# Sinkhorn attention, a two-axis FFT, layer norm and an MLP on one core: loads in need order, a second folding of the transform, a GpSimd power, and transposes by the DMA crossbar

## The chip, the cores and the metric

The kernel runs on one core of one Trainium2 chip. The metric is the device time in microseconds (us) of that core. Every kernel here is timed in rounds beside the kernel before, on the same chip (another chip in another call), and all runs of this study agree within about 0.8% for one kernel. One more execution of each is profiled. Its span, from the first to the last instruction, is 1 to 2 us shorter than the time.

The engines are called PE (TensorE, matrix products; its weight loads are shown apart as PEld), DVE (VectorE), ACT (ScalarE), POOL (GpSimd) and SP (SyncE). A "q" behind an engine's name is its sequencer, as it issues a transfer.

## The reference, cut to what matters

```python
def _attn_ref(q, k, v, sort_net):            # q, k, v: 4 batches, 8 heads, 768 rows, 64
    P = sort_net                             # 4 x 8 matrices of 8 x 8
    for _ in range(5):                       # Sinkhorn
        P = exp(P - max(P, -1)); P = P / sum(P, -1); P = P / sum(P, -2)
    k_sorted = einsum('bhij,bhjcd->bhicd', P, k_blocks)
    v_sorted = einsum('bhij,bhjcd->bhicd', P, v_blocks)
    return softmax(q_blocks @ k_sorted.T / 8) @ v_sorted   # inside each block of 96

def _moe_ref(x, w_ch1, w_ch2):               # x: 4 x 768 x 512
    mixed = real(fft(fft(x, axis=1), axis=2))
    u = x + mixed
    un = (u - mean(u)) / sqrt(var(u) + 1e-6) # over the 512 of a row
    return u + maximum(un @ w_ch1, 0) @ w_ch2   # 512 x 2048 and 2048 x 512
```

One batch goes through it in this order: Sinkhorn, sorting of k and v, attention, first FFT axis, second FFT axis ("tiles" u of 128 rows, six to a batch), norm, MLP.

## The kernel before, where the change and the argument touch it

The Python of the kernel runs a few generators (attention, FFT, MLP, v of the later batches). The framework then orders each engine's instructions by a priority. An engine works strictly in that order, so an instruction that waits holds back all that stand behind it on the same engine.

A table of the second axis, `lt`, has 97 rows. Its two copies are loaded, and each is followed by a load of the single row 96 of `rb`. The table of the v correction (`tab`, f32) is loaded after them.

```python
    for n in range(2):
        lt = const.tile([97, S], F16, name=f"lt{n}")
        nc.sync.dma_start(lt, cn["lt"].ap())                # 97 rows; row 96 is written later
        rb = const.tile([97, DM], F16, name=f"rb{n}")
        nc.sync.dma_start(rb[96:97, :], cn["rrow"].ap())    # one row
    # ... cut ...
    tab = cload("tab", [128, 2, 2, 257], F32)
```

The second axis is one accumulation per tile, four matmuls of 512 columns and one with `lt` and `rb`:

```python
            ps = pf([128, DM])
            nc.tensor.matmul(ps, lt[:, 128 * T:128 * T + 128], rb, start=True, stop=False)
            for c in range(4):
                lh = ys[c][g][:, 128 * tt:128 * tt + 128]
                rh = cdb[:, c, :] if c < 2 else sdb[:, c - 2, :]
                nc.tensor.matmul(ps, lh, rh, start=False, stop=(c == 3))
```

The norm's inverse root is an integer first guess on DVE and three Newton steps on POOL, 15 small operations. Each normalised tile `un` is transposed by four PE matmuls and copied out of PSUM. The mean of v of batches 2 and 3 is subtracted on DVE by eight operations of 0.87 us. k and q go through two buffers each, and POOL issues their loads, so a new load waits on POOL until the old k or q has been used.

The softmax here doesn't subtract the row's maximum and nothing guards it: scores larger than these inputs give would overflow.

## Time and profile before

| | us |
|---|---|
| time, median of 4 runs beside the kernel after | 371.64 (370.59 to 373.28) |
| span of the profiled execution | 369.3 |
| table `tab` lands | 64.8 |
| first FFT's first operation | 88.8 |
| first MLP matmul | 129.6 |

The page of the profile, its row of busy tenths in 40 equal slices (9 is 90% or more; PEclk is the clock granted to PE, in tenths of full speed):

```profile
PE   0989500864885789999998999998999999999995
...
PEclk9998955775589699999999999999999999999999
DMA  8999987060335100514001101000100100100102
```

The matrix engine is full from slice 15 on and has holes before. The windows of the same trace, cut where the MLP starts (columns: window, length, busy time and count of PE, PEld, DVE, ACT, POOL, then clock, DMA share, GB/s):

```profile
0.00:129.60 129.60, 75.43 (x761) 53.40 (x762) 76.70 (x184) 57.90 (x102) 19.41 (x47) 0.78 0.65 139
129.60:369.30 239.70, 229.95 (x1695) 132.63 (x1692) 144.08 (x324) 80.61 (x148) 24.25 (x108) 1.00 0.11 33
```

After 129.6 us PE is busy for 230 of 240 us. Before, it is busy for 75 of 130. What it waited for there is in its waits (us in total, how often, the longest):

```profile
PE pf_575 L508 <- DMA tab_sb<-k_tab: 23.1, 1, 23.1
PE pm_139 L252 <- DMA v_82<-in_v_dram: 9.8, 1, 9.8
PE pf_1268 L704 <- ACT un_1250 L692: 5.5, 1, 5.5
PE pf_870 L636 <- DVE ee_834 L620: 5.3, 1, 5.3
```

The largest is the wait for `tab`. The timeline of SP's issues (start, duration, what) tells why it comes so late:

```profile
27.48 0.24 SPq L240 DMA_DIRECT2D lt_129<-k_lt  x1
27.77 7.63 SPq L243 DMA_DIRECT2D rb_131<-k_rrow  x1
35.44 1.06 SPq L240 DMA_DIRECT2D lt_133<-k_lt  x1
36.55 14.09 SPq L243 DMA_DIRECT2D rb_135<-k_rrow  x1
50.68 0.34 SPq L144 DMA_DIRECT2D tab_sb<-k_tab  x1
```

Two issues of one row took 7.6 and 14.1 us, and `tab` stands behind them.

### The profile page before, as it was taken

What the parts mean: (1) busy time and instruction counts of PE and PEld (TensorE: products, weight loads), DVE (VectorE), ACT (ScalarE), POOL (GpSimd) and SP (SyncE); (2) the same over time, 40 slices, a digit from 0 to 9 for tenths busy, and PEclk for the clock granted to TensorE, in tenths of its full rate; (3) what the DMA queues carried; (4) which work ended last, traced back from release to release, by engine and by line L of the source; (5) the groups of instructions that cost most, each with busy time, mean ns of one, the idle gap of its engine ahead of it and who ended that gap; (6) DMA issues with size and microseconds to landing.
All of it is one profiled execution on the core that took longest, in us unless ns stands there. A gap on an engine that the chain in (4) does not pass through costs nothing.

```text
span 369.3 us, 6087 instructions
## 1 busy us (share of the span) xinstructions
PE 305.4 (83%) x2452; PEld 186.0 (50%) x2452; DVE 220.8 (60%) x507; ACT 138.5 (38%) x249; POOL 43.7 (12%) x155
## 2 busy tenths in 40 slices
PE   0989500864885789999998999998999999999995
PEld 0448400752543667666643555664455555454552
DVE  3477500399988596447986644579473286563542
ACT  1647600371648688715302585630124212022100
POOL 7111000010004104000012300002011020021000
PEclk9998955775589699999999999999999999999999
DMA  8999987060335100514001101000100100100102
GB/s 155 320 265 225 210 219 250 27 105 0 44 45 66 22 0 6 83 57 78 9 0 58 41 2 51 36 2 0 59 28 3 58 28 2 57 30 28 57 2 85
DMA packets 18477, 25.95 MB, mean 70 GB/s; under 512 B 1737, under 2 KB 12685, under 8 KB 18449
## 3 DMA queue, kind: packets, MB, share of 16 engines
q0 software_dynamic: 11136, 10.49, 18.3%
q1 hardware_dynamic: 7314, 15.08, 11.5%
q8 instruction: 19, 0.31, 0.4%
q14 instruction: 8, 0.07, 0.1%
HBM read 29.37 MB, written 6.29 MB: 97 GB/s over the span
## 4 chain that ended last, share of the span: by engine, by line
PE 57%; DVE 19%; DMA 12%; SPq 7%; issue 2%; ACT 2%; POOL 1%; DVEq 0%; ACTq 0%
SPq L243 6%; DMA vcx<-k_sdb 4%; DMA tab_sb<-k_tab 4%; DMA v_82<-in_v_dram 2%; DVE vcx L873 2%; PE pm_3075 L773 1%; DVE r_540 L425 1%; PE pm_3013 L773 1%; PE pf_575 L508 1%; PE pm_2172 L773 1%; PE pm_2918 L773 1%; PE pm_4212 L773 1%; PE pm_2322 L773 1%; PE pm_3791 L773 1%; PE pm_4039 L773 1%
## 5 line engine op out<-in xcount | busy, mean ns | idle before, releaser
L756 PEld LDWEIGHTS <-w1sb 128*128 128x128 f16 x512 | 49.2, 98 | 36.6 <-issue 5.1
L508 PE MATMUL pf_575<-tab_sb,atp_537 128*64 128x129 f32 (+1 forms) x16 | 3.7, 405 | 23.1 <-DMA tab_sb<-k_tab 23.1
L465 PEld LDWEIGHTS <-vcx 128*128 128x128 f16 x128 | 18.1, 181 | 5.4 <-issue 2.3
L165 DVE CAST vsf<-pm_502 96x512 f16<-96x512 f32 x1 | 0.8, 799 | 27.7 <-PE pm_502 L468 27.7
L252 PE MATMUL pm_139<-v_82,idf_sb 128*128 128x512 f32 x12 | 7.7, 812 | 9.8 <-DMA v_82<-in_v_dram 9.8
L508 PEld LDWEIGHTS pf_575<-tab_sb,atp_537 128*64 128x64 f32 x16 | 3.1, 218 | 23.4 <-issue 23.4
L163 ACT CAST vsf<-pm_492 96x512 f16<-96x512 f32 x1 | 0.8, 786 | 25.2 <-PE pm_492 L468 25.2
L252 PEld LDWEIGHTS pm_139<-v_82,idf_sb 128*128 128x128 f32 x12 | 3.1, 267 | 13.6 <-issue 12.5
L468 PEld LDWEIGHTS <-vbn 128*128 128x128 f16 x64 | 8.7, 136 | 0.7 <-DVE bdv_1_291 L440 0.7
L773 PEld LDWEIGHTS <-hr_4077 128*128 128x128 f16 x48 | 4.7, 98 | 5.5
L773 PEld LDWEIGHTS <-hr_2224 128*128 128x128 f16 x48 | 4.7, 98 | 5.6
L773 PEld LDWEIGHTS <-hr_3663 128*128 128x128 f16 x48 | 4.7, 98 | 5.5
L773 PEld LDWEIGHTS <-hr_1704 128*128 128x128 f16 x48 | 4.6, 98 | 5.2
L773 PEld LDWEIGHTS <-hr_3127 128*128 128x128 f16 x48 | 4.6, 98 | 5.1
L773 PEld LDWEIGHTS <-hr_3898 128*128 128x128 f16 x48 | 4.6, 98 | 5.1
L692 ACT ACTIVATE un_3291<-u_2960,nm_3108,ny_3106 128x512 f16<-128x512 f32 x1 | 0.8, 813 | 16.8 <-POOL nm_3108 L680 16.8
L368 PEld LDWEIGHTS <-ksb_109 64*128 64x128 f16 x128 | 3.8, 97 | 6.5 <-issue 4.3
L413 PEld LDWEIGHTS <-ebuf_101 97*128 97x128 f16 x96 | 5.7, 108 | 2.6 <-DVE ebuf_101 L390 2.0
L692 ACT ACTIVATE un_2388<-u_2057,nm_2205,ny_2203 128x512 f16<-128x512 f32 x1 | 0.8, 813 | 16.5 <-POOL nm_2205 L680 16.5
L260 ACT CAST vcx<-v_82 128x768 f16<-128x768 f32 x4 | 3.3, 832 | 9.7 <-DMA v_82<-in_v_dram 9.7
L773 PEld LDWEIGHTS <-hr_3365 128*128 128x128 f16 x48 | 4.6, 98 | 4.5
L773 PEld LDWEIGHTS <-hr_2467 128*128 128x128 f16 x48 | 4.2, 98 | 4.7 <-issue 0.2
(1428 smaller groups left out, 896.4 us busy)
## 6 DMA issues: line engine op xcount, KB each, us to landing
w1sb<-in_moe_w_ch_dram POOLq DMA_DIRECT2D x4, 512.0 KB, 23.4
w2sb<-in_moe_w_ch_dram POOLq DMA_DIRECT2D x4, 512.0 KB, 32.3
v_82<-in_v_dram SPq DMA_DIRECT2D x4, 384.0 KB, 6.6
v_83<-in_v_dram SPq DMA_DIRECT2D x4, 384.0 KB, 13.2
v_524<-in_v_dram SPq DMA_DIRECT2D x2, 768.0 KB, 18.0
v_527<-in_v_dram SPq DMA_DIRECT2D x2, 768.0 KB, 18.9
tab_sb<-k_tab SPq DMA_DIRECT2D x1, 514.0 KB
k_70<-in_k_dram POOLq DMA_DIRECT2D x1, 384.0 KB, 5.6
```

Of the source, the lines that this page charges most:

```text
L243: nc.sync.dma_start(rb[96:97, :], cn["rrow"].ap())
L252: nc.tensor.matmul(psm.rearrange("p c d -> p (c d)"), idf, v32[n // 6][:, 8 * (n % 6):8 * (n % 6) + 8, :].rearrange("p c d -> p (c d)"), s ...
L260: nc.scalar.copy(vcp[:, 2 * n:2 * n + 2], v32[hf][:, 12 * qq:12 * qq + 12, :].rearrange("p (c r) d -> p c r d", r=6))
L368: nc.tensor.matmul(pss[h2][:, j, :], ks[rows, 4 * g + j].rearrange("p r c -> p (r c)"), qt[rows, :, cc])
L413: nc.tensor.matmul(po[:, 65 * T:65 * T + 96], e[:, S * g + 256 * tt + 128 * n: S * g + 256 * tt + 128 * n + 128], vsf[:, vi:vi + 96], star ...
L425: nc.vector.tensor_tensor(rt[:, :, D * h:D * h + D], po3[:, :, 0:D], rz[:, :, None].broadcast_to([128, 6, D]), op=ALU.mult)
L465: nc.tensor.matmul(ps[:, dd, :], vcx[:, :, d], bd, start=True, stop=(t == 1))
L468: nc.tensor.matmul(ps[:, dd, :], vbn[:, d:d + 1].broadcast_to([128, 128]), bd, start=False, stop=True)
L508: nc.tensor.matmul(psr[64 * o:64 * o + 64, cs], atp[:, par, c].rearrange("p b g -> p (b g)"), tab[:, o, c, cs], start=(c == 0), stop=(c == 1))
L756: nc.tensor.matmul(ps, w1sb[:, c, 128 * fc:128 * fc + 128], ut[:, c, :], start=(c == 0), stop=(c == 3))
L773: nc.tensor.matmul(ps, hr[:, fc, 128 * tt:128 * tt + 128], w2sb[:, fc, :], start=(fc == 0), stop=(fc == 15))
L873: nc.vector.tensor_tensor(vcp[:, 2 * n:2 * n + 2], v1[hf][:, 12 * qq:12 * qq + 12, :].rearrange("p (c r) d -> p c r d", r=6), vbs[1][:, 0: ...
```

## The change

The change has one aim, an earlier start of the MLP and fewer columns after it.

- Loads stand in the order of need: `tab` directly after v, both `lt` in one load and both `rb` rows in one, w1 between the two k and q loads of batch 1 and w2 behind them, and v of batches 2 and 3 in two pieces from POOL. Many instructions are given to `start(...)`, which keeps them at their place in program order.
- The mean of those later batches of v is subtracted by matmuls instead of on DVE, as for the first two already. v only needs a cast (ACT) and a tree of sums (DVE).
- The second axis is folded once more. A fold uses the symmetry of cosine and sine: mirrored inputs are added and subtracted first (on DVE), so that half as many products are left. Now even and odd output columns come from two matmuls of 256 columns each.
- The inverse root is one `pow` on POOL. Four operations replace 15.
- Rows of batches 1 to 3 are transposed by the DMA crossbar (a transfer that transposes on its way) instead of PE.
- Batch 1's attention waits until both groups of batch 0 are normalised.

```diff
+    load_qk(0, 1)
...
-    for n in range(8):
-        hf, qq = divmod(n, 4)
-        nc.sync.dma_start(v32[hf][:, 12 * qq:12 * qq + 12, :],
-                          vv[0:128, 12 * n:12 * n + 12, :])
+    for n in range(4):
+        hf, qq = divmod(n, 2)
+        start(nc.sync.dma_start(v32[hf][:, 24 * qq:24 * qq + 24, :],
+                                vv[0:128, 24 * n:24 * n + 24, :]))
...
+    start(nc.sync.dma_start(tab, cn["tab"].ap()))
+    start(nc.sync.dma_start(dtab, cn["dtab"].ap()))
+    start(nc.sync.dma_start(cs, cn["cs"].ap()))
+    lt2 = const.tile([97, 2, S], F16, name="lt2")
+    start(nc.sync.dma_start(lt2, cn["lt"].ap()))
+    start(nc.sync.dma_start(rb2[96:97], ...))
...
-            x = wt([128, 3], F32, "nx", 2)
...          (integer guess on DVE, three Newton steps on POOL)
+            nc.gpsimd.tensor_scalar(mv[:, :, 1], mv[:, :, 1], 1e-6, None, op0=ALU.add)
+            nc.gpsimd.tensor_tensor(y, mv[:, :, 1], mhalf, op=ALU.pow)
+            nc.gpsimd.tensor_tensor(nm, mv[:, :, 0], y, op=ALU.mult)
+            nc.gpsimd.tensor_scalar(nm, nm, -1.0, None, op0=ALU.mult)
...
+                if b > 0:
+                    nc.sync.dma_start_transpose(ut[:, :, 128 * tt:128 * tt + 128], un)
+                    continue
...
             for c in range(4):
                 lh = ys[c][g][:, 128 * tt:128 * tt + 128]
-                rh = cdb[:, c, :] if c < 2 else sdb[:, c - 2, :]
-                nc.tensor.matmul(ps, lh, rh, start=False, stop=(c == 3))
+                nc.tensor.matmul(ps[:, c % 2::2], lh, dtab[:, c, :],
+                                 start=(c == 0), stop=False, skip_group_check=True)
+            nc.tensor.matmul(ps, lt[:, 128 * T:128 * T + 128], rb,
+                             start=False, stop=True, skip_group_check=True)
...
+    def v1_gen():                             # v of batches 2 and 3
+        for hf in range(2):
+            sv = wt([128, 48, D], F32, "hrB", 1, "v32")
+            start(nc.gpsimd.dma_start(sv, vv[128:256, 48 * hf:48 * hf + 48]))
+            while clk["PE"] < 62.0 + 8.0 * hf:      # a gate in the generators' model of time
+                yield None
+            for n in range(4):
+                v_cast(sv[:, 12 * n:12 * n + 12, :], 4 * hf + n)
+            ...      (tree of sums on DVE)
...
+    load_qk(1, 0)
+    for n in range(16):
+        v_mix(0, n)
+    for c in range(4):
+        start(nc.gpsimd.dma_start(w1sb[:, c, :], w1v[:, c, :]))
+    load_qk(1, 1)
+    for c in range(4):
+        start(nc.gpsimd.dma_start(w2sb[:, 4 * c:4 * c + 4, :], ...))
```

(`vv` holds four batches in two groups of 128 rows: the first is batches 0 and 1, the second batches 2 and 3. The texts below call the second group "v of batch 1" in places; its loads are v_530 and v_930.)

## The prediction

> **What bounds it now.** Two regimes. From 130 us to 365 us TensorE is nearly full: the windows from 130 to 370 show 222 us of PE busy, clock 1.00, and the chain of waits is almost only MLP matmuls (0.65 us per first-layer group, 0.216 us per 512-column matmul). Before 130 us PE is busy 84 us. The waits show PE idle 23.1 us (to 64.8) for the f32 table tab: the SP queue issues it only at 50.7, behind one-row loads whose issue took 7.6 and 14.1 us, while w1 was issued at 5.3. The clock is then 0.50 from 46 to 65. From 77 to 101 VectorE is full; the v reduction and mean subtraction of batches 2, 3 take about 14 us of it, on the path to the first FFT (88.8). The first layer norm takes 8 us from its first tiny op (113.4) to the last (121.2). The MLP starts at 129.8.
>
> The Trainium skill (DMA: Bandwidth & Descriptors, "Issuing engines are not separate DMA queues") says that DMAs of all issuers interleave on the same 16 engines. The trace agrees: DMA share is about 1.0 until 46 us while w1 and v both fly.
>
> **What changes.**
> - Need order: tab follows v, before 42 us; the 23 us hole goes. w1 is issued at about 35 us; at about 310 GB/s of reads (20.97 MB in 18.3% of the span) w1 lands near 54, w2 near 72, v's second half near 77 and 90: just in time.
> - The subtraction (8 x 0.87 us DVE) becomes ACT casts plus 64 PE matmuls (+4 us); DVE's 14 us leave the first FFT's path.
> - Folded axis: 4 x 512 columns become 4 x 256 per tile, 0.86 to 0.43 us: -10.3 us PE (-7.8 in the full stretch), for about +2 us DVE per batch.
> - pow: 15 small ops become 4; 8 us become 2, on the path only for batch 0.
> - DMA transposes: -72 PE transposes (-6.4 us PE), -18 evictions of 0.4 us; latency about 3 us (estimate: an output store's 2.0 us plus margin), hidden by two ut buffers.
> - Batch 1's attention waits for batch 0's norms: its 11 us of PE move after the MLP start.
>
> **Path sum.** First FFT 42 + 18 = 60 us; first DFT2 tile +10; three tiles +5; norm +2; transposes +4: the MLP starts near 80 (was 130). PE after it: 222 - 7.8 - 6.4 + 4 + 11 + 1 = 224 us, gaps 13 as now, tail 4: span 321 to 325, time 327.
>
> **Prediction.** 327 us, 8 in 10 within 313 to 345. Faster 0.95, same 0.03, slower 0.02. Nearly all of the gain is the head's (load order above all, then DVE); the folded axis, the transposes and the added mean matmuls nearly cancel with batch 1's moved attention.
>
> **What would show it.** Right: no PE wait over 5 us for tab; MLP's first matmul at 75 to 88; second-axis matmuls about 0.11 us each; PE over 90% busy from there; four GpSimd ops in under 2 us per norm; VectorE not full before the first FFT. Wrong: PE waiting for w1, w2 or v's second half after 80 (GpSimd holds w1 behind q/k buffers), or for ut over 5 us.
>
> **What would make it wrong.** Crossbar transposes of several us each, in a queue with output stores that wait for the MLP; pow much slower than what it replaces; v's second half after 100 us, which holds the second MLP group; 256-column matmuls paced by weight loads (98 ns, close to 108).

## More of the kernel before

The matmuls of one tile of the second axis, in the timeline of PE:

```profile
298.68 0.38 PE L725 MATMUL pf_3780<-vcx,yr_3539 128*128 128x512 f16 x1
298.90 0.38 PE L725 MATMUL pf_3780<-vcx,yr_3554 128*128 128x512 f16 x1
299.12 0.38 PE L725 MATMUL pf_3780<-vcx,yr_3569 128*128 128x512 f16 x1
```

Their starts are 0.22 us apart. That pitch, not the 0.38 us from start to modelled end, is what a matmul costs in a full stream.

## The result, and the profile after

The time after is 350.88 us, the median of 4 runs (350.21 to 352.11), beside 371.64. The ratio is 0.944, with a 95% interval from 0.940 to 0.949. A ratio is the mean time of one kernel's fast runs over that of the other's in the same rounds, so it is not quite the ratio of the medians. The execution that was profiled after the change was the slowest of the four (352.11). The kernel became faster, as predicted, but the time lies 24 us above the prediction and outside its range.

| us | before | predicted | after |
|---|---|---|---|
| end of the Sinkhorn (last cast starts on DVE) | 23.7 | not changed | 29.9 |
| first FFT's first operation | 88.8 | 60 | 65.8 |
| first tile of the second axis | 106 | 70 | 86.0 |
| last of the norm's small operations done | 121.4 | 77 | 93.8 |
| first MLP matmul | 129.6 | 80 | 99.2 |
| from there to the end | 239.7 | 241 | 251.1 |
| span | 369.3 | 321 to 325 | 350.3 |

So 19 us of the miss are in the start of the MLP and 10 in the stretch after it; the upper end of the predicted span is 325. The same rows of the page, after:

```profile
PE   1935996565379999999999999999999999999995
...
PEclk9985799576879999999999999999999999999999
DMA  7970099990130707060650020101112012112102
```

The windows, cut where the MLP starts now:

```profile
0.00:99.20 99.20, 61.38 (x506) 44.18 (x507) 54.49 (x134) 41.34 (x73) 17.86 (x35) 0.79 0.67 156
99.20:350.30 251.10, 243.58 (x1939) 144.28 (x1937) 151.56 (x318) 107.08 (x203) 19.59 (x36) 1.00 0.22 50
```

PE works longer in the second stretch than before (243.6 against 230.0 us), though the prediction had the work moved in and the work taken out nearly cancel (222 to 224). The waits of PE, in answer to those of before:

```profile
PE pm_174 L330 <- DVE pdup_170 L321: 10.0, 1, 10.0
PE pm_121 L262 <- DMA v_80<-in_v_dram: 7.5, 1, 7.5
PE pf_875 L730 <- ACT y_855 L658: 7.3, 1, 7.3
PE pf_952 L712 <- ACT un_949 L695: 5.2, 1, 5.2
PE pf_817 L647 <- DVE ee_808 L622: 4.0, 1, 4.0
```

The wait for `tab` is gone. Two of the waits at the top are new: for `pdup`, the Sinkhorn's result, and for `y`, the result of the first axis. SP's issues show the early `tab`, and a slow one-row issue that now has nothing urgent behind it:

```profile
4.88 0.35 SPq L243 DMA_DIRECT2D tab<-k_tab  x1
...
9.97 0.24 SPq L249 DMA_DIRECT2D lt_115<-k_lt  x1
12.40 12.02 SPq L251 DMA_DIRECT2D rb_117<-k_rrow  x1
```

Why the Sinkhorn is later: the timeline of DVE (in brackets the idle time before, and what ended it):

```profile
10.17 0.19 DVE L304 RECIPROCAL rs<-rs 32x8 f32<-32x8 f32 x1
21.56 0.36 DVE L283 COPY qr_186<-q_72 128x768 f16<-128x768 f16 x1 [11.20 <-DMA q_72<-in_q_dram]
21.84 0.35 DVE L283 COPY qr_213<-q_72 128x768 f16<-128x768 f16 x1
22.11 0.21 DVE L305 TENSOR_TENSOR pw<-pw,rs 32x64 f32<-32x64 f32 x1
```

The Sinkhorn needs no q. Its step at L305 only stands behind two copies of q in DVE's order, and q_72 lands at 21.5 us (at 10.5 before). Why `y` is late: the timelines of POOL (the loads) and ACT:

```profile
42.94 0.90 POOL L182 DMA_DIRECT2D k_340<-in_k_dram  x1 [35.34 <-PE pm_404 L478]
...
57.09 0.89 POOL L182 DMA_DIRECT2D k_508<-in_k_dram  x1 [10.36 <-PE pf_660 L355]
...
61.92 0.56 POOL L862 DMA_DIRECT2D v_530<-in_v_dram  x1
```

```profile
79.33 3.03 ACT L269 CAST vcx<-v_530 128x768 f16<-128x768 f32 x4 [6.41 <-DMA v_530<-in_v_dram]
82.27 0.48 ACT L658 ACTIVATE y_855<-pf_848 128x386 f16<-128x386 f32 x1
```

The casts of v_530 stand before `y_855`, which the first tile needs. Nothing before the MLP's second group needs them: that group takes over the buffer in which v_530 lies. ACT waits 6.4 us for v_530 and then casts for 3.0. v_530 is so late because POOL stands twice at a load of k that waits for a buffer (35.3 and 10.4 us), and everything that POOL issues later waits with it.

The second axis after, in the timeline of PE:

```profile
233.16 0.42 PE L730 MATMUL pf_3186<-vcx,yr_2621 128*128 128x256 f16 x1
233.37 0.42 PE L730 MATMUL pf_3186<-vcx,yr_2659 128*128 128x256 f16 x1
233.59 0.42 PE L730 MATMUL pf_3186<-vcx,yr_2676 128*128 128x256 f16 x1
```

A matmul of 256 columns has a pitch of 0.21 us, the same as one of 512 before. The fold gave nothing here. The shorter norm, on the contrary, is what was expected, the first of four operations starting at 91.97 and the `pow` taking 0.89 us:

```profile
92.29 0.89 POOL L681 TENSOR_TENSOR ny_910<-mv_874,mhalf 128x3 f32<-128x3 f32 x1
93.26 0.19 POOL L682 TENSOR_TENSOR nm_911<-mv_874,ny_910 128x3 f32<-128x3 f32 x1
93.55 0.25 POOL L683 TENSOR_SCALAR nm_911<-nm_911 128x3 f32<-128x3 f32 x1
```

### The profile page after: what moved, and what is told of

The parts are those of the page before. It is cut to its first block, busy times and chain, and to the rows that moved or that the text cites. A ratio compares the mean times of both kernels' runs of the same rounds, so it can differ in the third digit from the quotient of the medians.

```text
span 350.3 us, 5983 instructions
## 1 busy us (share of the span) xinstructions
PE 305.0 (87%) x2444; PEld 188.5 (54%) x2444; DVE 206.1 (59%) x452; ACT 148.4 (42%) x276; POOL 37.5 (11%) x71
## 3 DMA queue, kind: packets, MB, share of 16 engines
q0 software_dynamic: 11424, 13.63, 21.5%
## 4 chain that ended last, share of the span: by engine, by line
issue 51%; PE 24%; DMA 10%; POOL 7%; DVE 4%; ACT 2%; POOLq 0%; DVEq 0%
DMA v_530<-in_v_dram 5%; DMA k_70<-in_k_dram 4%; PE pm_3673 L786 1%; PE pm_4048 L786 1%; PE pm_4010 L786 1%; PE pm_3856 L786 1%; PE pm_3479 L786 1%; PE pm_4029 L786 1%; PE pm_3894 L786 1%; PE pm_3875 L786 1%; PE pm_3643 L786 1%; PE pm_3509 L786 1%; PE pm_3437 L786 1%; POOL w2sb L955 1%; ACT vcx L269 1%
## 5 line engine op out<-in xcount | busy, mean ns | idle before, releaser
L425 PEld LDWEIGHTS <-eb_87 97*128 97x128 f16 x384 | 19.6, 103 | 2.3 <-issue 1.1
L476 PEld LDWEIGHTS <-vcx 128*128 128x128 f16 x128 | 20.1, 172 | 1.1 <-issue 0.2
L262 PE MATMUL pm_121<-v_80,pack 128*128 128x512 f32 x12 | 7.9, 825 | 7.5 <-DMA v_80<-in_v_dram 7.5
L262 PEld LDWEIGHTS pm_121<-v_80,pack 128*128 128x128 f32 x12 | 3.1, 270 | 11.5 <-issue 11.5
L478 PEld LDWEIGHTS <-vbn_303 128*128 128x128 f16 x64 | 8.7, 137 | 0.4 <-issue 0.4
L478 PEld LDWEIGHTS <-vbn_965 128*128 128x128 f16 x64 | 8.3, 130 | 0.2
L870 DVE TENSOR_TENSOR v_530<-v_530 128x1536 f32<-128x1536 f32 (+2 forms) x3 | 3.3, 1088 | 7.7 <-ACT vcx L269 7.7
L786 PEld LDWEIGHTS <-hrB_3545 128*128 128x128 f16 x48 | 4.7, 98 | 5.5
L786 PEld LDWEIGHTS <-hrA_3749 128*128 128x128 f16 x48 | 4.7, 98 | 5.5
L786 PEld LDWEIGHTS <-hrA_3276 128*128 128x128 f16 x48 | 4.7, 98 | 5.6
L786 PEld LDWEIGHTS <-hrB_3913 128*128 128x128 f16 x48 | 4.7, 98 | 5.6
L786 PEld LDWEIGHTS <-hrB_3069 128*128 128x128 f16 x48 | 4.7, 98 | 5.4
L786 PEld LDWEIGHTS <-hrB_1521 128*128 128x128 f16 x48 | 4.6, 99 | 5.4 <-issue 0.2
L786 PEld LDWEIGHTS <-hrA_2438 128*128 128x128 f16 x48 | 4.5, 98 | 5.0
L786 PEld LDWEIGHTS <-hrA_999 128*128 128x128 f16 x48 | 4.4, 97 | 4.8
L296 ACT ACTIVATE pw<-pw 32x64 f32<-32x64 f32 x5 | 1.3, 254 | 12.4 <-DVE pw L305 12.3
## 6 DMA issues: line engine op xcount, KB each, us to landing
v_81<-in_v_dram SPq DMA_DIRECT2D x2, 768.0 KB, 11.9
```

The costliest lines, as they stand in the source:

```text
L262: nc.tensor.matmul(psm.rearrange("p c d -> p (c d)"), idf, v32[n // 6][:, 8 * (n % 6):8 * (n % 6) + 8, :].rearrange("p c d -> p (c d)"), s ...
L296: nc.scalar.activation(pw, pw, AF.Exp)
L425: nc.tensor.matmul(po[:, 65 * T:65 * T + 96], e[:, S * g + 256 * tt + 128 * n: S * g + 256 * tt + 128 * n + 128], vsf[:, vi:vi + 96], star ...
L476: nc.tensor.matmul(ps[:, dd, :], vcx[:, :, d], bd, start=True, stop=False)
L478: nc.tensor.matmul(ps[:, dd, :], vbn[t][:, d:d + 1].broadcast_to([128, 128]), bd, start=False, stop=True)
L786: nc.tensor.matmul(ps, hr[:, fc, 128 * tt:128 * tt + 128], w2sb[:, fc, :], start=(fc == 0), stop=(fc == 15))
```

## The experiments

Fourteen kernels ran. All gave the correct result. Times are medians; "ratio" is to the kernel before in the same rounds (0.944 for the kernel after). In the traces of these runs line numbers are shifted by a few. My theory was that four things explain the 24 us: the order on ACT and DVE behind late loads (q in the Sinkhorn, v before `y`), the strided output of the folded matmuls, the idle DMA queue behind k's buffers, and 97-row loads. The rival for each was that its wait stands beside another of the same length, so that nothing is won by removing it.

Two limits hold for all that follows. The kernel after was not run again in these calls, so "less than the kernel after" compares calls; its own ratio is known to about 1.7 us, and differences of 2 us or less are not resolved. And in the traces with unchanged early loads, DVE's first copy of q starts anywhere from 19.8 to 21.9 us, so that a start of the MLP is comparable to about 2 us.

### b_lt96: the kernel before, without the 97th row

```diff
-        nc.sync.dma_start(lt, cn["lt"].ap())
+        nc.sync.dma_start(lt[0:96], cn["lt"].ap()[0:96])
```

> The kernel before, with the two lt tables loaded as 96 rows instead of 97 (row 96 is written by the kernel anyway); every engine keeps its order. Theory S (97 and 1 rows put a whole load on one of the 16 DMA engines, and the SP queue stands behind it): the two rb issues of 7.6 and 14.1 us shrink to about 1 us, tab is issued near 29 us instead of 50.7 and lands by 42, PE's 23 us wait for tab falls under 4 us, and the time falls by 15 to 23 us, to 349 to 357. Rival L (tab is late because w1 and w2 were issued first and fill all 16 engines): tab still lands after 55, and the time falls by less than 6 us.

Measured: 355.80 us (354.89 to 356.90), ratio 0.957 [0.954, 0.960]. The issues of `rb` take 0.28 us each, `tab` is issued at 29.25 us, the wait for it is gone, and the MLP starts at 113.2:

```profile
28.24 0.28 SPq L243 DMA_DIRECT2D rb<-k_rrow  x1
28.57 0.30 SPq L240 DMA_DIRECT2D lt<-k_lt  x1
28.92 0.28 SPq L243 DMA_DIRECT2D rb<-k_rrow  x1
29.25 0.34 SPq L144 DMA_DIRECT2D tab_sb<-k_tab  x1
```

So the order of the engines' instructions and of the loads can stay as it was, and 16.5 us (372.31 less 355.80, against the kernel before in these rounds) of the change's 20.8 come from leaving out one row that the kernel overwrites anyway. Not only `tab` comes earlier: the first load of v of batches 2 and 3 behind it is issued at 29.7 us instead of 51.2. The Trainium skill explains it ("DMA: Bandwidth & Descriptors", section "Why a DMA increments its semaphore by 16 and not by 1", "How many engines"): a transfer is spread over the largest number of engines up to 16 that divides the slowest dimension larger than 1 of both sides, which is 16 for 96 rows and, by that rule, 1 for 97. The traces agree, with the issue of the next load at 7.6 and 14.1 us behind 97 rows and at 0.28 us behind 96; the next run shows the single engine itself.

### a_lt96: the same edit in the kernel after

```diff
-    start(nc.sync.dma_start(lt2, cn["lt"].ap()))
+    start(nc.sync.dma_start(lt2[0:96], cn["lt"].ap()[0:96]))
```

> The changed kernel with lt loaded as 96 rows instead of 97; every engine keeps its order. Theory V (the first q tile lands at 21.5 us instead of 10.5 because v's rows, now 6 KB instead of 3 KB, take more of each engine's turns): q_72 still lands at 20 to 22, only the one-engine tail from 24 to 40 us and the late q_76 (33.8) go; the time stays within 1.5 us of 350.9. Theory S (the one-engine load of lt also holds the q and k loads): q_72 lands before 17 and the time falls by 4 to 8 us.

Measured: 352.08 us (351.47 to 352.20), ratio 0.947 [0.945, 0.949]; no gain. The slow trickle of DMA between 26 and 35 us (21 GB/s in that slice of the page after) falls to nothing, as the same window of 4 us shows, first in the kernel after, then here:

```profile
28.00:32.00 4.00, 1.39 (x14) 1.39 (x14) 3.74 (x13) 1.04 (x1) 0.00 (x0) 0.50 0.07 20
28.00:32.00 4.00, 1.52 (x15) 1.52 (x15) 3.75 (x12) 1.04 (x1) 0.00 (x0) 0.50 0.00 0
```

A DMA share of 0.07 is about one engine of 16 (0.06), so the load of 97 rows ran on one. But the Sinkhorn ends at 29.75 as before, and the MLP starts at 98.3. In the kernel after nothing that matters stands behind the 97 rows any more. The 97 rows are not the cause of the late q.

### a_v8: v of batches 0 and 1 in eight pieces instead of four

```diff
-    for n in range(4):
-        hf, qq = divmod(n, 2)
-        start(nc.sync.dma_start(v32[hf][:, 24 * qq:24 * qq + 24, :], vv[0:128, 24 * n:24 * n + 24, :]))
+    for n in range(8):
+        hf, qq = divmod(n, 4)
+        start(nc.sync.dma_start(v32[hf][:, 12 * qq:12 * qq + 12, :], vv[0:128, 12 * n:12 * n + 12, :]))
```

> The changed kernel with v of batches 0 and 1 in eight pieces of 3 KB rows instead of four of 6 KB, as before the change. Theory V: k_70 and q_72 land near 10 and 15 us (21.5 now), the Sinkhorn chain ends near 24 to 26 instead of 29.4, the first score matmuls come 4 to 6 us earlier, and the time falls by 3 to 6 us. If the turn of each engine doesn't depend on the row length, q_72 stays at 20 to 22 and the time within 1.5 us.

Measured: 348.29 us (346.65 to 348.89), ratio 0.936 [0.933, 0.939]. DVE's copy of q starts at 16.3 instead of 21.6, the first FFT at 60.75 instead of 65.8. The wait for `y` becomes longer (8.6 us), which takes back part, and the MLP starts at 94.8. So the pieces of 6 KB per row are about half of q's delay of 11 us; the rest, from the other loads that now go out earlier beside it, was not separated. The skill's page "DMA: Bandwidth & Descriptors" says in "Queues, rings and completion order" that an engine takes turns between queues a packet at a time. The run fits that, but it shows only the effect of the size, not the turns.

### a_castpin: v's casts and sums kept behind batch 0's first axis

```diff
+        if pin:
+            start(i)                                     # in v_cast
-            while clk["PE"] < 62.0 + 8.0 * hf:
+            while clk["PE"] < 66.0 + 8.0 * hf:
-                v_cast(sv[:, 12 * n:12 * n + 12, :], 4 * hf + n)
+                v_cast(sv[:, 12 * n:12 * n + 12, :], 4 * hf + n, True)
-                nc.vector.tensor_tensor(sv[:, 0:w], ...)
+                start(nc.vector.tensor_tensor(sv[:, 0:w], ...))
```

> The changed kernel with the casts and the tree adds of v's second half (batches 2 and 3) pinned in ScalarE's and VectorE's order behind the two y evictions of the first FFT; the loads keep their order and times. Theory C (ScalarE, in program order, sits on a cast whose v tile lands at 79.3 us, while the FFT's evictions wait behind it): PE's 7.3 us wait for y goes, the first MLP matmul comes at 88 to 93 instead of 99.2, and the time falls by 6 to 11 us, to 340 to 345. Rival: the first half of MLP then waits for w2 or for v's halves anyway, and under 3 us are gained.

Measured: 342.12 us (341.69 to 343.57), ratio 0.921 [0.918, 0.924], 8.8 us less than the kernel after. ACT now makes `y` first, at 70.0 to 73.2 us, and the casts still wait for the same late v:

```profile
72.70 0.49 ACT L660 ACTIVATE y<-pf 128x386 f16<-128x386 f32 x1 [0.21 <-PE pf L649]
79.57 3.03 ACT L269 CAST vcx<-v 128x768 f16<-128x768 f32 x4 [6.38 <-DMA v<-in_v_dram]
84.13 1.52 ACT L697 ACTIVATE un<-u,nm,ny 128x512 f16<-128x512 f32 x2 [1.53 <-POOL nm L685]
```

v lands no earlier. The place in ACT's order cost the time, not the lateness of the load. The first MLP matmul comes at 89.5. Not all of the wait is gone: PE waits 6.9 us at the transposes for `un` (5.2 in the kernel after). This is no longer the casts, which are done at 82.6; ACT then waits 1.5 us for POOL's `nm`, the last small operation of the norm:

```profile
82.47 1.62 POOL L685 TENSOR_SCALAR nm<-nm 128x3 f32<-128x3 f32 x1
```

The same operation took 0.25 us in the kernel after (93.55). It runs here beside DVE's first f32 sum of v (82.20 to 83.99). In six more traces, the second norm of the kernel after among them, it takes 1.67 to 1.81 us, each time beside such a sum; why was not tested.

### a_w1first: w1 and w2 ahead of the k and q of batch 1

```diff
+    for c in range(4):
+        start(nc.gpsimd.dma_start(w1sb[:, c, :], ...))
+    for c in range(4):
+        start(nc.gpsimd.dma_start(w2sb[:, 4 * c:4 * c + 4, :], ...))
     load_qk(1, 0)
     for n in range(16):
         v_mix(0, n)
     load_qk(1, 1)
```

> The changed kernel with w1 and w2 issued in GpSimd's queue before the q and k of batch 1, whose buffers are free only after batch 0's k was used (42.9 and 57.1 us). Theory D (the DMA engines idle from 24 to 44 us because w1 stands behind those loads, and the whole backlog, v's second half last, arrives 15 us late): DMA share stays near 1 from 24 us on, v's first half of batches 2 and 3 lands at 62 to 69 us instead of 79.3, PE's 7.3 us wait for y goes, time falls by 6 to 11 us, to 340 to 345. Rival: the early w1 takes turns from q, tab and cs, as before the change, so the first scores come later and under 3 us are gained.

Measured: 357.53 us (356.84 to 358.00), ratio 0.961 [0.959, 0.964]. It is 6.6 us slower than the kernel after. The idle stretch of the queue is filled, and it does harm. Batch 1's q now comes behind 4 MB of weights, and its copy stands in DVE's order before batch 0's work: DVE waits 12.2 us for it (and 11.8 for batch 0's q), PE 10.2 us for DVE's `vsf` behind it. v is issued even later (68.4 us), since k's second buffer still waits for PE. My theory that the idle queue was the cause is refuted in this form.

### a_w1mid: only w1 ahead

```diff
+    for c in range(4):
+        start(nc.gpsimd.dma_start(w1sb[:, c, :], ...))
     load_qk(1, 0)
     ...
+    w2's four loads
     load_qk(1, 1)
```

> The kernel after with only w1 (not w2) issued before the k and q of batch 1's first half. Theory (the queue stands idle from 24 to 44 us behind a buffer of k and q, so w1 can go there for nothing and everything behind it, v of batch 1 too, comes some 10 us earlier): v's first half lands at 66 to 71 instead of 79.3, the wait of PE at L714 or L730 for the scalar engine's y shrinks from 7.3 to below 2 us, 342 to 346 us. Rival (as when w1 and w2 both went first: batch 1's q copy stands in the vector engine's order before work of batch 0 and waits for its load): vector engine waits over 15 us at the q copy, 352 us or more.

Measured: 348.79 us (348.38 to 349.10), ratio 0.939 [0.937, 0.941]; 2.1 us gained, at the edge of what is resolved, and not 5 to 9. v lands 10 us earlier, at 69.2, and the wait for `y` is gone. But PE waits 11.7 us a step earlier, for `ee`, the fold of the first axis on DVE: with the earlier v, DVE's sum of v stands before it and waits 6.3 us for ACT's cast. The wait was moved, not removed.

### a_nofold: the second axis with one fold again

```diff
-                nc.tensor.matmul(ps[:, c % 2::2], lh, dtab[:, c, :],      # 256 columns
+                nc.tensor.matmul(ps, lh, dtab[:, c, :],                   # 512 columns
```

(The tables and the DVE folds that feed it are also those of before.)

> The changed kernel with the second axis unfolded again (four matmuls of 512 columns per tile, no second fold on VectorE). If PE is full from the MLP start, the 18 tiles after it cost 18 x 0.43 = 7.7 us more, and the first six are paid on the path of batch 0 too (up to 2 us at half clock), less 2 us of VectorE before batch 0's second axis: time rises by 6 to 10 us, to 357 to 361. If the fold was hidden or paid back on VectorE, it changes by under 2 us.

Measured: 349.23 us (348.48 to 350.74), ratio 0.940 [0.937, 0.943]. It is not slower without the fold; the 1.7 us by which it is faster are not resolved. PE's second stretch is as long as with it (250.7 against 251.1 us, PE busy 243.2 against 243.6). The head runs in another order here: PE waits 14.2 us for `un` and no longer for `y`. The fold as written gave nothing.

### a_foldc: the two halves side by side in PSUM

```diff
-            ps = pf([128, DM])
+            ps = pf([128, 2, DM // 2])
-                nc.tensor.matmul(ps[:, c % 2::2], lh, dtab[:, c, :], ...)
+                nc.tensor.matmul(ps[:, c % 2, :], lh, dtab[:, c, :], ...)
-            nc.tensor.matmul(ps, lt[...], rb, ...)
+            nc.tensor.matmul(ps, lt[...], rb.rearrange("p (m n) -> p n m", n=2), ...)
-            nc.vector.scalar_tensor_tensor(u, rt[:, T, :], RSC, ps, ...)
+            nc.vector.scalar_tensor_tensor(u.rearrange(il, n=2), rt[:, T, :].rearrange(il, n=2),
+                                           RSC, ps.rearrange("p n m -> p m n"), ...)
```

> The kernel after with the two 256-column halves of the second axis written side by side in PSUM (columns 0-255 and 256-511) instead of interleaved; the interleaving is done where the vector engine reads the sum. The count of matmul columns is the same. Theory P (the strided write to PSUM sets the 0.215 us of a 256-column matmul): its pitch falls to about 0.11 us, the 96 of them give back up to 10 us of the TensorE's stage less what becomes weight-load bound, 342 to 346 us. Rival (something else paces these matmuls, such as the weight loads between them): the pitch stays at 0.2 us and the time within 1.5 us of 350.9. Third possibility: the pitch falls but the vector engine's permuted read takes what was won.

Measured: 342.68 us (342.14 to 343.38), ratio 0.923 [0.920, 0.925], 8.2 us less than the kernel after. Four matmuls now take as long as two did, in the timeline of PE from the first of four to the one after them:

```profile
224.96 0.60 PE L730 MATMUL pf<-vcx,yr 128*128 128x256 f16 x4
225.39 0.39 PE L733 MATMUL pf<-rb,lt 97*128 97x512 f16 x1
```

That is 0.43 us for four, 0.107 each. The count of columns and the weight loads are those of the kernel after; only where a column is written in PSUM differs (and the order in which `rb` and the sum are read). So the pitch of 0.21 us was the price of writing every second 4-byte column. DVE's read across the two halves costs nothing to see (a mean of 685 ns for an operation of L739; 0.69 us for the first one in the kernel after). The second stretch is 5.3 us shorter (245.8 us). The rest came before it: in the profiled execution the MLP starts 4.6 us sooner (94.6), with a q that came 1.6 us sooner.

### a_qpin: the q copies behind the Sinkhorn

```diff
-        nc.vector.tensor_copy(qr, ...)
+        i = nc.vector.tensor_copy(qr, ...)
+        if b == 0 and hp < 2:
+            start(i)
```

> The kernel after with the vector engine's copies of batch 0's first two q tiles kept behind the Sinkhorn steps in its order. Theory (the Sinkhorn waits only because these copies stand before it and their q lands at 21.5 us): the wait of 11.2 us for q_72 leaves the Sinkhorn, its end comes 2 to 5 us sooner than 29.9, the MLP starts up to as much earlier, 346 to 350 us. Rival (the Sinkhorn is late for v's sums, which its own loads set, or what is won is given back at the k and q of the first scores, which land at 15.1 and 21.5): Sinkhorn end within 1 us of 29.9 or the FFT's first add within 1 us of 65.8, time within 1.5 us of 350.9.

Measured: 345.51 us (344.82 to 347.09), ratio 0.931 [0.928, 0.934], 5.4 us less than the kernel after. The cast at the Sinkhorn's end starts at 20.4 instead of 29.9 us, and PE's wait for it shrinks from 10.0 to 1.4. The MLP starts at 92.2. No load was touched; again only the order mattered.

### a_petr: batches 1 to 3 transposed by PE again

```diff
-                if b > 0:
+                if b > 9:
```

> The changed kernel with all normalised rows transposed on PE again. If PE's time is what counts: 72 transposes and their 18 evictions come back, 4 to 7 us slower, 355 to 358. If the crossbar's latency and the output stores in the same queue cost waits of their own, the difference is under 2 us or even negative.

Measured: 354.41 us (353.92 to 354.90), ratio 0.953 [0.951, 0.956]. The crossbar's transposes are worth 3.5 us. PE's time in the second stretch rises by 3.5 us (247.1 against 243.6). PE does not wait for a crossbar transpose in the kernel after, and in its variants by 2.8 us at most (a_nopow). ACT waits for one before it may overwrite `un`, 1.9 us at most in the kernel after; in a_nofold DVE waits 5.3 us.

### a_nopow: the Newton steps again

```diff
-            nc.gpsimd.tensor_tensor(y, mv[:, :, 1], mhalf, op=ALU.pow)
+            (integer guess on DVE; x -0.5 and three Newton steps of four operations on POOL)
```

> The kernel after with the power on GpSimd replaced by the Newton steps of before. The prediction counted 6 us on the first norm (8 to 2 us) and nothing later. If that is right: 355 to 358 us, the MLP's start about 6 us later than 99.2. Rival (the first norm is not on the chain, because the next tiles or the casts hold PE there anyway): within 2 us of 350.9.

Measured: 358.90 us (358.12 to 358.96), ratio 0.965 [0.962, 0.967]. The power is worth 8.0 us. But the place is not the expected one: the MLP starts at 101.0, only 1.8 us later than with the power (with a q that came 1.2 us sooner), and the stretch after it is 5.0 us longer (256.1 against 251.1), with PE waits of 2.6 to 2.8 us for `un` and `ut` that the kernel after does not have. The first norm's small operations take 4.6 us here (90.9 to 95.5 in the trace), not the 8 us of the kernel before. There the first 3.9 us went by before the Newton steps proper: the three small steps on DVE (113.4, 115.3, 116.8 us) stood between other work of DVE. The framework placed many other instructions differently in this run, so the split between the two stretches is less certain than the sum.

### a_best1: four mends together, with w1 and w2 first

a_lt96, a_v8, a_castpin and the order of a_w1first in one kernel.

> All four repairs of the head together: lt as 96 rows, v in eight pieces, w1 and w2 ahead of batch 1's q and k, v's second casts and adds pinned behind the first FFT's evictions. If the error of the prediction was the head alone, the first MLP matmul comes at 80 to 87 us and the time is 329 to 338; if PE's work after it was underestimated as well, it stays above 340.

Measured: 344.59 us (344.06 to 345.15), ratio 0.926 [0.923, 0.929]; missed, and slower than a_castpin alone. The MLP starts at 92.7, and DVE waits 6.9 us for batch 1's q (and 11.9 for batch 0's). The order of a_w1first accounts for it: the single effects of a_v8, a_castpin and a_w1first (-2.6, -8.8 and +6.6) add up to 346.1.

### a_best2: all mends, with only w1 first

a_lt96, a_v8, a_castpin, a_foldc, a_qpin and a_w1mid in one kernel.

> All together: 96 rows of lt, v in 8 pieces, q copies behind the Sinkhorn, w1 alone before batch 1's first k and q, casts and sums of batch 1's v pinned at the gate of 66 us, contiguous PSUM halves. If the single gains add up (castpin -9, v8 -2.9, foldc -6, qpin and w1mid some -3 together): 326 to 333 us. If the gains of the head overlap (each shortens the same wait): 334 to 338. If w1 ahead of batch 1's k and q does harm as it did with w2: over 338.

Measured: 325.36 us (324.68 to 326.17), ratio 0.875 [0.873, 0.878]. It beats both kernels, and the MLP starts at 79.4 us.

### a_best3: the same without a_w1mid

```diff
-    for c in range(4):
-        start(nc.gpsimd.dma_start(w1sb[:, c, :], ...))      # back behind load_qk(1, 0)
```

> The version of 325.4 us with w1 put back to its place of the kernel after (issued after batch 1's first k and q). If w1 ahead of the k and q only mattered because v's casts stood in order before batch 0's work (now they are pinned behind a later gate), its place is worth nothing now: within 1.5 us of 325.4. If the idle stretch of the queue still binds, because v of batch 1 comes late and PE then waits at the vector engine's v as in the pinned version (6.9 us): 328 to 334.

Measured: 325.42 us (324.96 to 326.19, 5 runs), ratio 0.876 [0.874, 0.878]. The place of w1 is worth nothing once the casts are pinned. The windows of this run:

```profile
0.00:78.30 78.30, 53.53 (x506) 39.04 (x507) 55.00 (x135) 41.88 (x72) 19.26 (x35) 0.83 0.84 184
78.30:323.40 245.10, 235.28 (x1939) 141.29 (x1937) 149.74 (x315) 107.72 (x206) 18.39 (x36) 0.99 0.23 56
```

The MLP starts at 78.3, where the prediction had 80. PE still waits 7.8 us before it, at the transposes of the first `un`, so a few more us lie there.

## Why the prediction was wrong

The direction was right, and the wait for `tab` was the largest piece (whether it took a new load order to remove it is in point 7). The size was wrong by 24 us. Of the 19 us at the MLP's start, 5.8 came before the first FFT, 10.2 between it and the first tile, and 3.2 after that. The single mends add up to the whole. From 350.88, a_castpin takes 8.8 us, a_foldc 8.2, a_qpin 5.4 and a_v8 2.6, together 25.0. All of them together, with a_lt96, measured 25.5 (350.88 less 325.42); each number is good to 1 or 2 us only. So the waits stood one behind the other, not beside each other.

1. **"First FFT 42 + 18 = 60 us": 65.8.** The prediction assumed that nothing ahead of 42 us moves. It had noted that the transfers of all issuers share the same engines, and it did not apply this to q, which now flies beside larger pieces of v, `tab` and the tables. q landed 11 us later, and two q copies stood before the Sinkhorn in DVE's order. They had stood there in the kernel before, where DVE waited 6.3 us for that q (10.5), so the profile before showed the place. a_qpin and a_v8 show both causes.
2. **"First DFT2 tile +10; v's second half near 77 and 90: just in time": the first tile came 20 us after the FFT's start.** The load was estimated well, 79.3 against 77. What failed is "just in time": the step asked when the MLP needs v and not what stands behind the casts in ACT's order. `y` did, so a load that only the MLP's second group needed held the first tile by 7.3 us of PE wait. a_castpin shows it, with an unchanged landing. The second piece, issued on POOL behind the first norm, came at 100.8 against 90, past the 100 us that the prediction had named as a danger; no wait of PE comes from it. "w1 is issued at about 35 us" was wrong as well (44.6), because k's buffers hold POOL, but a_best3 shows that this costs nothing once the casts are pinned.
3. **"Folded axis, 0.86 to 0.43 us: -10.3 us PE": 0.86 to 0.85.** The prediction counted columns read, not the step at which they are written. The page that it needed was there: the skill's "PSUM — Partial Sum Buffer", section "Specifications (TRN2)", says of the 8-byte cachelines that any non-contiguous access pattern slows matmuls significantly. Here the slowing is a factor of two, 0.21 against 0.107 us (a_foldc), which cancels the fold (a_nofold). The danger that the prediction did name, a pace set by weight loads of 98 ns, did not come true: the contiguous form runs at 0.107. That is what the skill's "TensorE: Matmul & The Clock Gate", section "Back-to-back issue gap", gives for 256 columns with its isolated formula (an estimate of 109 ns).
4. **"PE busy after it 222": an error of reading.** The windows add up to 230, not 222 us, and those before 130 us to 75.8, not 84, which is their sum up to 140. The text also took 13 us of gaps and 4 of tail, where the measured gaps after are 7.5 in all. The two errors cancel to a few us, so the sum was closer than its terms. PE's work before the MLP fell by 14.0 us (75.4 less 61.4), where batch 1's attention was taken for 11. As an estimate, with the fold at zero and the transposes at the 3.5 us of a_petr, 230.0 + 14.0 - 3.5 + 4 makes 244.5; measured were 243.6.
5. **"pow: 8 us become 2": right for the trace, wrong as an account.** The operations took 1.8 us, and the power is worth 8.0 us (a_nopow). But of the 8 us before, only 4.1 were the Newton chain on POOL (117.3 to 121.4); the rest was the order on DVE, which the earlier schedule alone changes. And by a_nopow's trace most of the gain (5.0 us of 6.8) lies in the stretch after the MLP's start, which the prediction put off the path.
6. **"-72 PE transposes, -6.4 us": right in kind, 3.5 us in the time** (a_petr). No wait of PE for the crossbar appeared, as predicted.
7. **"Load order above all".** True of the waits, but b_lt96 shows that 16.5 of the 20.8 us are had without any reordering. The prediction read "one-row loads whose issue took 7.6 and 14.1 us" and blamed the place of the loads. It did not ask why an issue of one row should take 14 us.

Not tested alone: the mean matmuls in place of DVE's subtraction, and the holding back of batch 1's attention. What they gave is only argued.

## What to carry to other kernels

When a load is moved, look not only at when its data is needed but at the instruction that touches it first: on an engine that works in order, a cast placed too early puts a load that nothing urgent needs on the critical path, and moving the load only moves the wait. Cost a matmul by how it writes PSUM as well as by its columns, and make the written columns contiguous, leaving the interleaving to the engine that reads them. If the issue of a small transfer takes several us, look at the one before it on the same queue: the count of its rows may leave it with a single engine.

## What the Trainium skill lacked or had wrong

- "PSUM — Partial Sum Buffer" ("Specifications (TRN2)") gives no size for "slows matmuls significantly". Here an f16 matmul of 256 columns with an f32 output at every second column has a pitch of 0.21 us, against 0.107 with contiguous columns. The first is the pitch of 512 contiguous columns (0.22).
- "TensorE: Matmul & The Clock Gate" ("Back-to-back issue gap") says that in a stream of weight loads and matmuls the spacing is about 131 ns for 512 columns and that the isolated 216 ns over-counts. In these traces, a stream of pairs of weight load and 512-column matmul at full clock runs at 0.22 us (298.68, 298.90, 299.12 in the kernel before; 15 of the MLP's second layer in 3.24 us). The isolated formula holds for 512 and for 256 columns.
- "DMA: Bandwidth & Descriptors" has the rule for the number of engines, but not what it costs the issuer: behind a load of 97 rows, the issue of a single row on the same queue took 7.6 to 14.1 us, behind 96 rows 0.28. In "Issuing engines are not separate DMA queues" it calls the time to initiate a DMA "usually small relative to the DMA itself"; here two such issues held `tab` for 21.7 us (7.63 + 14.09).
- No page that I found states the time of a `pow` on GpSimd: 128x3 f32 took 0.89 us, where a multiplication of the same shape took 0.19.
